# Chunk 1's inputs by sequence among the weights, block 0's state products together, and one output tile for each sequence at the end

## The chip, the cores and the metric

The kernel runs on one core of one Trainium2 chip. The metric is the device time of one execution in microseconds (us). The span of a profile is about 1.7 us shorter than the time of the same run.

Engine names: PE is TensorE (matmuls; PEld its weight loads), DVE is VectorE, ACT is ScalarE, POOL is GpSimd, SPq is SyncE's queue, which issues most DMAs.

## The reference

A chunked state-space scan (batch 4, 8 heads, 768 positions, head size 32, state size 16), whose output is the input of a feed-forward layer with the activation `h * cos(h)`:

```python
for c in range(nc):
    cum = np.cumsum(la, axis=-1)
    L = np.exp(cum[:, :, :, None] - cum[:, :, None, :]) * causal
    M = np.einsum('bhin,bhjn->bhij', Cc, Bc) * L
    y[:, :, sl] = M @ xc + (Cc @ state) * exp(cum)        # shortened
    state = decay_full * state + sum_j(Bx * decay_from_j) # shortened
...
h = x @ w_in            # (3072, 256) x (256, 2048)
g = h * np.cos(h)
return g @ w_out        # (2048, 256)
```

## The kernel before

The kernel cuts the 768 positions into 6 blocks ("chunks") of 128, each with 4 sequences. After a short prologue that scans block 0 alone, 96 steps follow, 16 for each block. In step n PE computes `hp` n (a slice of h for all four sequences), then `o` n-2 (the second matmul of the step two before). ACT and DVE make `gT` out of `hp` in between: k (ACT), w (DVE), sine (ACT), gT (DVE). The scan of the next block is woven into the steps: for each sequence `turn` (two transposes on PE, their copies cT and bcT on ACT, one product on DVE), `intra` (PE's g, DVE's m) and `finish` (PE's y, the yT copy on ACT, and the state). The weights come as words of 8 bytes and are put together on the chip in 16 pieces: `grade` (ACT and POOL), `join` (DVE and POOL).

Every engine works through its own queue in order. The two PSUM pools that matter are `bank(..., "h")` with 2 buffers for `hp`, and `pair(...)` with 2 buffers of two banks each for the scan.

```python
def load(c, each=False):                       # B, C and x of one block
    ...
    for b in range(NB if each else 1):
        ...
        for dst, src in ((bc[:, 0, rs], B), (bc[:, 1, rs], C), (xr[:, rs], x)):
            nc.sync.dma_start(out=dst, in_=src[bs, :, sl, :].rearrange("b h s n -> s (b h) n"))
...
def carry(c, b):                               # the state after block c, sequence b
    if c == NC - 1:
        return
    xr, sc = raw[c][1], scaled.pop((c, b))
    s_ps = pair("s_ps")[:, 0, 0:2 * D]         # one PSUM buffer for each sequence
    for q in range(4):
        PE.matmul(s_ps[32 * q:32 * q + 32], ...)
    state[c, b] = new = states.tile(...)
    V.tensor_tensor(out=new..., in0=s_ps..., in1=own..., op=ALU.mult)
    ...
def second(n):                                 # at the very end:
    ...
    if last:                                   # o[c] is two tiles of two sequences
        for b in range(NB):
            ob = two.tile([P, DM], FP32, tag="ob1", bufs=NB, name="ob")
            (ACT.copy if b == 1 else V.tensor_copy)(out=ob, in_=o[c][b // 2][:, b % 2])
            (nc.scalar if b % 2 else nc.sync).dma_start(out=rows_[:, b, c, :], in_=ob)
        return
...
load(1)                                        # all of chunk 1 ahead of pieces 6 to 15
load_along(1)
for b in range(NB):
    load_a(1, (b,))
    for n in (6 + 2 * b, 7 + 2 * b):
        fetch(*order[n])
...
for n in range(NC * NF + LAG):
    ...
        first(n)
        if n + 3 < len(order):
            rest = grade(*order[n + 3], later=True)
        if n + 2 < len(order):
            join(*order[n + 2])
        for b in ((0,), (1, 2), (3,))[n] if n < 3 else ():
            carry(0, b)
        gate(n)
    ...
```

Of the kernel before, what the change touches and what calls it, by code (L numbers as in the profile page):

```python
# [8 lines left out]
FP32 = mybir.dt.float32  # L9
# [16 lines left out]
def kernel(  # L26
# [22 lines left out]
    nc = tc.nc  # L49
    V, ACT, G, PE = nc.vector, nc.scalar, nc.gpsimd, nc.tensor  # L50

    NB, H, S, D = x.shape
    N = B.shape[-1]
    P = 128
    NC = S // P
    DM, DF = moe_w_in.shape
    KT = DM // P
    NF = DF // P
# [8 lines left out]
    loads = ctx.enter_context(tc.tile_pool(name="loads", bufs=3))  # L67
    rows = ctx.enter_context(tc.tile_pool(name="rows", bufs=NB))
# [10 lines left out]
    def bank(shape, name, tag):  # L79
        return psum.tile(shape, FP32, tag=tag, bufs=2, name=name)  # L80

    def pair(name):

        return psum.tile([P, 2, 4 * P], FP32, tag="scan", bufs=2, name=name)
# [13 lines left out]
    a_all = dram.tile([NB, H, S], FP32, name="a_all")  # L98
    a_cut = dram.tile([NB, H, S], FP32, name="a_cut")

    def load(c, each=False):

        if c >= NC:
            return
        sl = slice(c * P, (c + 1) * P)
        bc = loads.tile([P, 2, NB * H, N], FP32, tag="bc", name="bc")
        xr = loads.tile([P, NB * H, D], FP32, tag="xr", name="xr")
        for b in range(NB if each else 1):
            bs = slice(b, b + 1) if each else slice(0, NB)
            rs = slice(bs.start * H, bs.stop * H)  # L110
            for dst, src in ((bc[:, 0, rs], B), (bc[:, 1, rs], C), (xr[:, rs], x)):
                nc.sync.dma_start(out=dst, in_=src[bs, :, sl, :].rearrange("b h s n -> s (b h) n"))  # L112
        raw[c] = (bc, xr.rearrange("p (b h) d -> p b h d", b=NB))

    def load_a(c, seqs=range(NB)):
        if c >= NC:
            return
        for b in seqs:
            arow[c, b] = t = rows.tile([P, H, P], FP32, tag="arow", name="arow")
            nc.sync.dma_start(  # L120
                out=t, in_=a_cut[b, :, c * P:(c + 1) * P].unsqueeze(0).to_broadcast([P, H, P]))

    def load_along(c):

        if c >= NC:
            return
        along[c] = t = rows.tile([P, NB, P], FP32, tag="along", bufs=2, name="along")
        for b in range(NB):
            nc.sync.dma_start(  # L129
                out=t[:, b], in_=a_all[b, :, c * P:(c + 1) * P].unsqueeze(1)  # L130
                .to_broadcast([H, N, P]))


# [65 lines left out]
                        in1=last.rearrange("p (k f) -> p k f", k=k), op=ALU.add)  # L199

    order = [(w, i) for i in range(NPC) for w in ("in", "out")]
    load(0, each=True)
    for n in (0, 2, 1, 3, 4, 5):
        fetch(*order[n])

# [110 lines left out]
    def finish(c, b, tag=None, fills=0):  # L316
        (bcT, m), xr = part.pop((c, b)), raw[c][1]
        y = (pair("y")[:, 0] if tag is None else bank([P, 4 * P], "y", tag)
             ).rearrange("p (k i) -> p k i", k=4)
        fill(y[:, 2:4], fills)  # L320
        y = y[:, 0:2]
        if c > 0:
            s = state[c - 1, b].rearrange("p h d -> p (h d)")
            for t in range(2):
                PE.matmul(y[:, t], lhsT=s[:, t * P:(t + 1) * P], rhs=bcT[:, 1],  # L325
                          start=(t == 0), stop=False, skip_group_check=True)
        for h in range(H):
            q, t = h % 4, h // 4
            PE.matmul(y[32 * q:32 * q + 32, t], lhsT=xr[:, b, h], rhs=m[:, h],  # L329
                      start=(c == 0 and t == 0), stop=True, tile_position=(0, 32 * q),  # L330
                      skip_group_check=True)
        if b == 0:
            yT[c] = two.tile([P, 2, TB], FP32, tag="yT", name="yT")
        ACT.copy(out=yT[c][:, :, b * P:(b + 1) * P], in_=y)  # L334
        if c > 0:
            carry(c, b)

    def carry(c, b):

        if c == NC - 1:  # L340
            return
        xr, sc = raw[c][1], scaled.pop((c, b))
        s_ps = pair("s_ps")[:, 0, 0:2 * D]
        for q in range(4):
            two_ = slice(2 * q, 2 * q + 2)
            PE.matmul(s_ps[32 * q:32 * q + 32], lhsT=sc[:, two_].rearrange("p h n -> p (h n)"),  # L346
                      rhs=xr[:, b, two_].rearrange("p h d -> p (h d)"), start=True, stop=True,
                      tile_position=(0, 32 * q), skip_group_check=True)
        state[c, b] = new = states.tile([P, H, D], FP32, tag="state", name="state")
        by_two = "p (k t) d -> p k (t d)"  # L350
        V.tensor_tensor(out=new.rearrange(by_two, k=HP),
                        in0=s_ps.unsqueeze(1).to_broadcast([P, HP, 2 * D]),
                        in1=own.rearrange(by_two, k=HP), op=ALU.mult)
        if c > 0:
            V.scalar_tensor_tensor(out=new, in0=state.pop((c - 1, b)),
                                   scalar=reach[c, b][:, P - 1:P], in1=new,
                                   op0=ALU.mult, op1=ALU.add)


    hp, turns, gT, o = {}, {}, {}, {}  # L360

    def first(n):
        c, f = divmod(n, NF)
        hp[n] = bank([P, TB], "hp", "h")
        for k in range(KT):
            PE.matmul(hp[n], lhsT=w_in[:, k, f * P:(f + 1) * P], rhs=yT[c][:, k],  # L366
                      start=(k == 0), stop=(k == KT - 1))

        k = ffn.tile([P, TB], I32, tag="k", name="k")
        ACT.activation(k, hp[n], AF.Copy, bias=0.25, scale=INV_2PI)  # L370
        turns[n] = w = ffn.tile([P, TB], FP32, tag="w", name="w")
        V.scalar_tensor_tensor(out=w, in0=hp[n], scalar=INV_2PI, in1=k,  # L372
                               op0=ALU.mult, op1=ALU.subtract)
# [7 lines left out]
    def second(n):  # L381
        c, f = divmod(n, NF)
        last = c == NC - 1
        if f == 0:

            o[c] = [pair("o")[:, :, 0:DM] if last else bank([P, 2, DM], "o", "o")
                    for _ in range(2)]
        g = gT.pop(n)
        for b in range(NB):
            PE.matmul(o[c][b // 2][:, b % 2], lhsT=g[:, b * P:(b + 1) * P],  # L390
                      rhs=w_out[:, f], start=(f == 0 and (last or b % 2 == 0)),
                      stop=(f == NF - 1), skip_group_check=True)
        if f < NF - 1:
            return
        rows_ = out.rearrange("(b c p) m -> p b c m", b=NB, p=P)
        if last:
            for b in range(NB):
                ob = two.tile([P, DM], FP32, tag="ob1", bufs=NB, name="ob")
                (ACT.copy if b == 1 else V.tensor_copy)(out=ob, in_=o[c][b // 2][:, b % 2])
                (nc.scalar if b % 2 else nc.sync).dma_start(out=rows_[:, b, c, :], in_=ob)  # L400
            return
        for i in range(2):
            ob = two.tile([P, 2, DM], FP32, tag="ob", name="ob")
            (ACT.copy if i else V.tensor_copy)(out=ob, in_=o[c][i])
            nc.sync.dma_start(out=rows_[:, 2 * i:2 * i + 2, c, :], in_=ob)


# [29 lines left out]
    fill(pair("warm")[:, 0, 0:2 * P].rearrange("p (k i) -> p k i", k=2), 1)  # L437
    join(*order[2])
    join(*order[1])
    load(1)  # L440
    load_along(1)
    for b in range(NB):
        load_a(1, (b,))
        for n in (6 + 2 * b, 7 + 2 * b):
            fetch(*order[n])
# [4 lines left out]
    for n in range(NC * NF + LAG):  # L450
        c, f = divmod(n, NF)
        rest = None
        if n < NC * NF:
            if f == 0 and c > 0:
                load(c + 2)
            first(n)
            if n + 3 < len(order):
                rest = grade(*order[n + 3], later=True)
            if n + 2 < len(order):
                join(*order[n + 2])  # L460
            for b in ((0,), (1, 2), (3,))[n] if n < 3 else ():
                carry(0, b)
            gate(n)
            if rest:
                rest()
        if n >= LAG:
            second(n - LAG)
        if c + 1 < NC:
            b, j = divmod(f - 3, 3)
            if 0 <= b < NB:  # L470
                (turn, intra, finish)[j](c + 1, b)
                if j == 0:
                    decays(c + 1, b, 1)
            b, j = divmod(f - 2, 3)
            if 0 <= b < NB and j == 0:
                reaches(c + 1, b)
                decays(c + 1, b, 0)
            if f == NF - 1:
                raw.pop(c + 1)
                load_a(c + 2)  # L480
                load_along(c + 2)
# [30 lines left out]
```

## Time and profile before

| | before |
|---|---|
| time, median of 6 runs | 410.89 us (410.28 to 411.93) |
| span of the profile | 408.7 us |
| PE busy | 400.2 us, 98% |
| all waits of PE | 4.4 us, none after 41 us |
| from PE's end to the end of the span (the tail) | 4.1 us |

A row of a timeline is: start, duration, engine, line, operation, output and inputs, number of instructions, and in brackets the idle time just before and what ended it. `x4` for one `hp` are its passes. The lines that carry the argument stand in the prediction below.

To compare traces I use times from the start of `hp` 0 on, the first matmul of the 96 steps: what comes before is the same in both kernels but, as the runs show, not equally long in each execution.

### The profile page before, as it was taken

What the parts mean: (1) busy time and instruction counts of PE and PEld (TensorE: products, weight loads), DVE (VectorE), ACT (ScalarE), POOL (GpSimd) and SP (SyncE); (2) the same over time, 40 slices, a digit from 0 to 9 for tenths busy, and PEclk for the clock granted to TensorE, in tenths of its full rate; (3) what the DMA queues carried; (4) which work ended last, traced back from release to release, by engine and by line L of the source; (5) the groups of instructions that cost most, each with busy time, mean ns of one, the idle gap of its engine ahead of it and who ended that gap; (6) DMA issues with size and microseconds to landing.
All of it is one profiled execution on the core that took longest, in us unless ns stands there. A gap on an engine that the chain in (4) does not pass through costs nothing.

```text
span 408.7 us, 5526 instructions
## 1 busy us (share of the span) xinstructions
PE 400.2 (98%) x2086; PEld 262.1 (64%) x2086; DVE 267.1 (65%) x413; ACT 173.3 (42%) x328; POOL 42.7 (10%) x62
## 2 busy tenths in 40 slices
PE   8989999999999999999999999999999999999995
PEld 5636666666666766666666666666666566666664
DVE  6997999955767754777763777674576764443332
ACT  2575566534343434343344433433434343433331
POOL 2263555400000000000000000000000000000000
PEclk9999999999999999999999999999999999999999
DMA  7999994191111093110155111120100000100001
GB/s 113 303 160 298 390 180 131 47 135 54 51 52 53 0 148 84 55 36 15 54 107 75 58 47 51 51 73 6 54 0 2 0 0 2 51 0 2 0 1 52
DMA packets 106507, 30.54 MB, mean 75 GB/s; under 512 B 75184, under 2 KB 102384, under 8 KB 106480
## 3 DMA queue, kind: packets, MB, share of 16 engines
q1 hardware_dynamic: 105664, 29.66, 30.8%
q10 hardware_dynamic: 816, 0.52, 0.4%
q8 instruction: 16, 0.26, 0.3%
q14 instruction: 11, 0.09, 0.1%
HBM read 26.84 MB, written 3.34 MB: 74 GB/s over the span
## 4 chain that ended last, share of the span: by engine, by line
PE 92%; SPq 4%; DMA 1%; ACT 1%; DVE 0%; issue 0%; DVEq 0%; ACTq 0%
PE hp L366 40%; PE o L390 39%; PE g L307 4%; PE y L329 3%; SPq L112 2%; PE y L325 2%; PE a_ps L256 2%; DMA words<-in_moe_w_in_dram 1%; SPq L129 1%; PE warm L94 1%; PE tp L289 1%; PE tp L288 1%; ACT cT L293 0%; PE s_ps L346 0%; DVE lam L272 0%
## 5 line engine op out<-in xcount | busy, mean ns | idle before, releaser
L366 PE MATMUL hp<-yT,w_in 128*128 128x512 f32 x384 | 184.9, 604 | 0.5 <-DVE gT L379 0.5
L390 PEld LDWEIGHTS o<-w_out,gT 128*128 128x128 f32 x768 | 145.8, 190 | 59.6 <-issue 43.5
L390 PE MATMUL o<-w_out,gT 128*128 128x256 f32 x768 | 181.2, 379 | 0.0
L370 ACT ACTIVATE k<-hp 128x512 int32<-128x512 f32 x96 | 57.4, 597 | 126.6 <-PE hp L366 126.5
L379 DVE TENSOR_TENSOR gT<-hp,w 128x512 f32<-128x512 f32 x96 | 66.3, 690 | 66.1 <-ACT w L377 66.1
L372 DVE SCALAR_TENSOR_TENSOR w<-hp,k 128x512 f32<-128x512 f32 x96 | 66.0, 687 | 62.5 <-ACT k L370 61.2
L366 PEld LDWEIGHTS hp<-yT,w_in 128*128 128x128 f32 x384 | 67.8, 190 | 57.5 <-issue 53.7
L377 ACT ACTIVATE w<-w,quarter 128x512 f32<-128x512 f32 x96 | 69.3, 722 | 75.9 <-DVE w L372 75.9
L272 DVE TENSOR_TENSOR_SCAN lam<-arow,unit 128x512 f32<-128x512 f32 x40 | 48.4, 1211 | 0.8 <-DMA arow<-a_cut 0.8
L311 DVE TENSOR_TENSOR m<-g,lam 128x512 f32<-128x512 f32 x48 | 30.7, 681 | 0.8 <-PE g L307 0.6
L281 POOL TENSOR_TENSOR sc<-bc,lam 128x128 f32<-128x128 f32 x20 | 8.2, 412 | 200.4 <-DVE lam L272 196.4
L307 PE MATMUL g<-cT,bcT 32*128 32x256 f32 x192 | 17.4, 426 | 1.9 <-ACT bcT L295 1.9
L293 ACT ACTIVATE cT<-tp,slot 128x128 f32<-128x128 f32 x48 | 14.6, 356 | 9.3 <-PE tp L289 9.3
L329 PE MATMUL y<-m,xr 128*32 128x128 f32 x384 | 15.8, 279 | 0.2 <-DVE m L311 0.2
L307 PEld LDWEIGHTS g<-cT,bcT 32*128 32x128 f32 x192 | 7.8, 182 | 9.5 <-issue 6.2
L194 DVE SCALAR_TENSOR_TENSOR mag<-words,mag 128x512 uint32<-128x512 uint32 x16 | 13.5, 842 | 0.6
L334 ACT COPY yT<-y 128x256 f32<-128x256 f32 x24 | 8.9, 371 | 11.1 <-PE y L329 11.1
L174 POOL TENSOR_SCALAR mag<-mag 128x512 f32<-128x512 f32 x16 | 12.1, 755 | 12.8 <-ACT mag L173 12.7
L173 ACT ACTIVATE mag<-words 128x512 f32<-128x512 f32 x16 | 11.0, 685 | 4.4 <-DMA words<-in_moe_w_in_dram 4.4
L325 PEld LDWEIGHTS y<-bcT,state 128*128 128x128 f32 x80 | 12.0, 191 | 1.3 <-DVE m L311 0.3
L325 PE MATMUL y<-bcT,state 128*128 128x128 f32 x80 | 12.3, 276 | 0.0
L329 PEld LDWEIGHTS y<-m,xr 128*32 128x32 f32 x384 | 8.9, 109 | 4.3 <-DVE m L311 1.4
(48 smaller groups left out, 153.2 us busy)
## 6 DMA issues: line engine op xcount, KB each, us to landing
arow<-a_cut SPq DMA_DIRECT2D x20, 512.0 KB
words<-in_moe_w_in_dram SPq DMA_DIRECT2D x8, 512.0 KB
words<-in_moe_w_out_dram SPq DMA_DIRECT2D x8, 512.0 KB
xr<-in_x_dram SPq DMA_DIRECT2D x5, 512.0 KB
out_dram<-ob SPq DMA_DIRECT2D x10, 256.0 KB
bc<-in_B_dram SPq DMA_DIRECT2D x5, 256.0 KB
bc<-in_C_dram SPq DMA_DIRECT2D x5, 256.0 KB
along<-a_all SPq DMA_DIRECT2D x20, 64.0 KB
```

What stands on the lines that cost most here:

```text
L272: V.tensor_tensor_scan(out=lam[c, b][:, hs].rearrange("p h i -> p (h i)"), data0=rows_.rearrange("p h i -> p (h i)"), data1=unit.rearrange ...
L293: ACT.activation(cT[:, t], tp[:, 1], AF.Copy, scale=slot[:, t:t + 1])
L307: PE.matmul(g[u // 2][:, u % 2, 0:2 * P], lhsT=bcT[r, 0], rhs=cT[r].rearrange("p t i -> p (t i)"), start=True, stop=True)
L311: V.tensor_tensor(out=m[:, hs].rearrange("p (k t) i -> p k (t i)", k=2), in0=g[u][:, :, 0:2 * P], in1=l[:, hs].rearrange("p (k t) i -> p k ...
L325: PE.matmul(y[:, t], lhsT=s[:, t * P:(t + 1) * P], rhs=bcT[:, 1], start=(t == 0), stop=False, skip_group_check=True)
L329: PE.matmul(y[32 * q:32 * q + 32, t], lhsT=xr[:, b, h], rhs=m[:, h], start=(c == 0 and t == 0), stop=True, tile_position=(0, 32 * q), skip ...
L366: PE.matmul(hp[n], lhsT=w_in[:, k, f * P:(f + 1) * P], rhs=yT[c][:, k], start=(k == 0), stop=(k == KT - 1))
L370: ACT.activation(k, hp[n], AF.Copy, bias=0.25, scale=INV_2PI)
L372: V.scalar_tensor_tensor(out=w, in0=hp[n], scalar=INV_2PI, in1=k, op0=ALU.mult, op1=ALU.subtract)
L377: ACT.activation(cos, cos, AF.Sin, bias=quarter, scale=TWO_PI)
L379: V.tensor_tensor(out=gT[n], in0=hp.pop(n), in1=cos, op=ALU.mult)
L390: PE.matmul(o[c][b // 2][:, b % 2], lhsT=g[:, b * P:(b + 1) * P], rhs=w_out[:, f], start=(f == 0 and (last or b % 2 == 0)), stop=(f == NF ...
```

## The change

The intent: take away two of the waits that PE still had near the start, and shorten the tail. In three parts, cut to the core:

```diff
 # part 1: state products of block 0 together, two sequences in each PSUM buffer
+    def sum_up(c, b, s_ps):                   # the matmuls that carry() held
+        ...
+        sums[c, b] = s_ps
     def carry(c, b):
-        s_ps = pair("s_ps")[:, 0, 0:2 * D]
-        for q in range(4): ...
+        s_ps = sums.pop((c, b))
 ...
             first(n)
+            if n == 1:
+                for b in range(0, NB, 2):
+                    s_ps = pair("s_ps")
+                    for t in range(2):
+                        sum_up(0, b + t, s_ps[:, t, 0:2 * D])
 ...
-            for b in ((0,), (1, 2), (3,))[n] if n < 3 else ():
+            for b in ((0, 1), (2, 3))[n - 1] if 0 < n < 3 else ():
                 carry(0, b)

 # part 2: chunk 1 by sequence among the weights
-    load(1)
-    load_along(1)
     for b in range(NB):
+        load(1, (b, b + 1))
+        load_along(1, (b,))
         load_a(1, (b,))
         for n in (6 + 2 * b, 7 + 2 * b):
             fetch(*order[n])

 # part 3: the last block's output, one PSUM tile for each sequence,
 # copied right after that sequence's matmuls, all issued from SyncE
+            if last:
+                o[c] = [pair("o")[:, 0, 0:DM] for _ in range(2)]
+            o_ = o_full[c] = [bank([P, 2, DM], "o", "o") for _ in range(2)]
+            o[c] = (o[c] + [t[:, 0] for t in o_] if last else ...)
 ...
         for b in range(NB):
             PE.matmul(o[c][b], ...)
+            if last and f == NF - 1:
                 ob = two.tile([P, DM], FP32, tag="ob1", bufs=NB, name="ob")
-                (ACT.copy if b == 1 else V.tensor_copy)(out=ob, in_=o[c][b // 2][:, b % 2])
-                (nc.scalar if b % 2 else nc.sync).dma_start(out=rows_[:, b, c, :], in_=ob)
+                (ACT.copy if b % 2 else V.tensor_copy)(out=ob, in_=o[c][b])
+                nc.sync.dma_start(out=rows_[:, b, c, :], in_=ob)
```

More of the change, by code (lines that the diff above doesn't have):

```diff
@@ L99, with load @@
     a_cut = dram.tile([NB, H, S], FP32, name="a_cut")
-    def load(c, each=False):
+    def load(c, seqs=(0, NB)):
         if c >= NC:
             return
-        sl = slice(c * P, (c + 1) * P)
-        bc = loads.tile([P, 2, NB * H, N], FP32, tag="bc", name="bc")
-        xr = loads.tile([P, NB * H, D], FP32, tag="xr", name="xr")
-        for b in range(NB if each else 1):
-            bs = slice(b, b + 1) if each else slice(0, NB)
-            rs = slice(bs.start * H, bs.stop * H)
-            for dst, src in ((bc[:, 0, rs], B), (bc[:, 1, rs], C), (xr[:, rs], x)):
-                nc.sync.dma_start(out=dst, in_=src[bs, :, sl, :].rearrange("b h s n -> s (b h) n"))
-        raw[c] = (bc, xr.rearrange("p (b h) d -> p b h d", b=NB))
+        if c not in raw:
+            raw[c] = (loads.tile([P, 2, NB * H, N], FP32, tag="bc", name="bc"),
+                      loads.tile([P, NB, H, D], FP32, tag="xr", name="xr"))
+        bc, xr = raw[c]
+        xr = xr.rearrange("p b h d -> p (b h) d")
+        rs = slice(seqs[0] * H, seqs[1] * H)
+        for dst, src in ((bc[:, 0, rs], B), (bc[:, 1, rs], C), (xr[:, rs], x)):
+            nc.sync.dma_start(out=dst, in_=src[seqs[0]:seqs[1], :, c * P:(c + 1) * P, :]
+                              .rearrange("b h s n -> s (b h) n"))
     def load_a(c, seqs=range(NB)):
@@ L121, in load_a, with load_along @@
                 out=t, in_=a_cut[b, :, c * P:(c + 1) * P].unsqueeze(0).to_broadcast([P, H, P]))
-    def load_along(c):
+    def load_along(c, seqs=range(NB)):
         if c >= NC:
             return
-        along[c] = t = rows.tile([P, NB, P], FP32, tag="along", bufs=2, name="along")
-        for b in range(NB):
+        if c not in along:
+            along[c] = rows.tile([P, NB, P], FP32, tag="along", bufs=2, name="along")
+        for b in seqs:
             nc.sync.dma_start(
-                out=t[:, b], in_=a_all[b, :, c * P:(c + 1) * P].unsqueeze(1)
+                out=along[c][:, b], in_=a_all[b, :, c * P:(c + 1) * P].unsqueeze(1)
                 .to_broadcast([H, N, P]))
@@ L201 @@
     order = [(w, i) for i in range(NPC) for w in ("in", "out")]
-    load(0, each=True)
+    for b in range(NB):
+        load(0, (b, b + 1))
     for n in (0, 2, 1, 3, 4, 5):
@@ L334, in finish @@
         ACT.copy(out=yT[c][:, :, b * P:(b + 1) * P], in_=y)
-        if c > 0:
+        if 0 < c < NC - 1:
+            sum_up(c, b, pair("s_ps")[:, 0, 0:2 * D])
             carry(c, b)
-    def carry(c, b):
-        if c == NC - 1:
-            return
+    sums = {}
+    def sum_up(c, b, s_ps):
         xr, sc = raw[c][1], scaled.pop((c, b))
-        s_ps = pair("s_ps")[:, 0, 0:2 * D]
         for q in range(4):
@@ L348, in carry @@
                       tile_position=(0, 32 * q), skip_group_check=True)
+        sums[c, b] = s_ps
+    def carry(c, b):
+        s_ps = sums.pop((c, b))
         state[c, b] = new = states.tile([P, H, D], FP32, tag="state", name="state")
@@ L357, in carry @@
                                    op0=ALU.mult, op1=ALU.add)
-    hp, turns, gT, o = {}, {}, {}, {}
+    hp, turns, gT, o, o_full = {}, {}, {}, {}, {}
     def first(n):
@@ L384, in second @@
         if f == 0:
-            o[c] = [pair("o")[:, :, 0:DM] if last else bank([P, 2, DM], "o", "o")
-                    for _ in range(2)]
+            if last:
+                o[c] = [pair("o")[:, 0, 0:DM] for _ in range(2)]
+            o_ = o_full[c] = [bank([P, 2, DM], "o", "o") for _ in range(2)]
+            o[c] = (o[c] + [t[:, 0] for t in o_] if last else
+                    [t[:, i] for t in o_ for i in range(2)])
         g = gT.pop(n)
+        rows_ = out.rearrange("(b c p) m -> p b c m", b=NB, p=P)
         for b in range(NB):
-            PE.matmul(o[c][b // 2][:, b % 2], lhsT=g[:, b * P:(b + 1) * P],
+            PE.matmul(o[c][b], lhsT=g[:, b * P:(b + 1) * P],
                       rhs=w_out[:, f], start=(f == 0 and (last or b % 2 == 0)),
                       stop=(f == NF - 1), skip_group_check=True)
-        if f < NF - 1:
-            return
-        rows_ = out.rearrange("(b c p) m -> p b c m", b=NB, p=P)
-        if last:
-            for b in range(NB):
+            if last and f == NF - 1:
                 ob = two.tile([P, DM], FP32, tag="ob1", bufs=NB, name="ob")
-                (ACT.copy if b == 1 else V.tensor_copy)(out=ob, in_=o[c][b // 2][:, b % 2])
-                (nc.scalar if b % 2 else nc.sync).dma_start(out=rows_[:, b, c, :], in_=ob)
+                (ACT.copy if b % 2 else V.tensor_copy)(out=ob, in_=o[c][b])
+                nc.sync.dma_start(out=rows_[:, b, c, :], in_=ob)
+        if last or f < NF - 1:
             return
@@ L403, in second @@
             ob = two.tile([P, 2, DM], FP32, tag="ob", name="ob")
-            (ACT.copy if i else V.tensor_copy)(out=ob, in_=o[c][i])
+            (ACT.copy if i else V.tensor_copy)(out=ob, in_=o_full[c][i])
             nc.sync.dma_start(out=rows_[:, 2 * i:2 * i + 2, c, :], in_=ob)
```

## The prediction

> **What bounds the kernel now.** I read the page's busy table first: TensorE (PE) is the engine to look at.
>
> ```profile
> PE 400.2 (98%) x2086; PEld 262.1 (64%) x2086; DVE 267.1 (65%) x413; ACT 173.3 (42%) x328; POOL 42.7 (10%) x62
> ```
>
> The waits of PE come next. They are all it ever waited for in 408.7 us; the windows say that none lies after 41 us (PE is busy 309.00 of the 309.00 us from 90 to 399), so that the middle of the kernel can't be shortened by moving instructions.
>
> ```profile
> PE g L307 <- ACT bcT L295: 1.9, 3, 0.9
> PE warm L94 <- DVE quarter L210: 1.1, 1, 1.1
> PE s_ps L346 <- DVE state L351: 0.7, 1, 0.7
> PE hp L366 <- DVE gT L379: 0.5, 1, 0.5
> PE y L329 <- DVE m L311: 0.2, 1, 0.2
> ```
>
> Together 4.4 us, and 4.1 us of tail after PE's end at 404.6. Then PE's timeline in the stretch that the change touches; the columns are start, duration, what, and the idle time just before.
>
> ```profile
> 22.41 1.95 PE L366 MATMUL hp<-yT,w_in 128*128 128x512 f32 x4
> 24.30 0.32 PE L346 MATMUL s_ps<-xr,sc 128*32 128x64 f32 x8
> 24.55 1.98 PE L366 MATMUL hp<-yT,w_in 128*128 128x512 f32 x4
> 26.46 0.43 PE L346 MATMUL s_ps<-xr,sc 128*32 128x64 f32 x16
> 27.36 1.95 PE L366 MATMUL hp<-yT,w_in 128*128 128x512 f32 x4 [0.46 <-DVE gT L379]
> 30.01 0.32 PE L346 MATMUL s_ps<-xr,sc 128*32 128x64 f32 x8 [0.70 <-DVE state L351]
> 30.26 1.99 PE L390 MATMUL o<-w_out,gT 128*128 128x256 f32 x8
> 32.09 1.88 PE L366 MATMUL hp<-yT,w_in 128*128 128x512 f32 x4
> ...
> 37.47 1.89 PE L390 MATMUL o<-w_out,gT 128*128 128x256 f32 x8
> 40.10 1.03 PE L307 MATMUL g<-cT,bcT 32*128 32x256 f32 x8 [0.74 <-ACT bcT L295]
> ```
>
> The reader is to see two holes: the fourth sequence's state product (30.01) has no free PSUM buffer until VectorE (DVE) has read the earlier ones, and the first `o` stands behind it; and the first g of chunk 1 (40.10) waits for ScalarE (ACT). ACT's timeline says why ACT is late:
>
> ```profile
> 37.51 0.69 ACT L173 ACTIVATE mag<-words 128x512 f32<-128x512 f32 x1 [2.85 <-DMA words<-in_moe_w_in_dram]
> ```
>
> and the SyncE queue why those words are late: their issue stands behind the whole of chunk 1.
>
> ```profile
> 17.25 7.01 SPq L112 DMA_DIRECT2D bc<-in_C_dram  x1
> 24.31 2.39 SPq L112 DMA_DIRECT2D xr<-in_x_dram  x1
> 26.80 4.29 SPq L129 DMA_DIRECT2D along<-a_all  x4
> 31.13 0.46 SPq L120 DMA_DIRECT2D arow<-a_cut  x1
> 31.64 1.13 SPq L159 DMA_DIRECT2D words<-in_moe_w_in_dram  x1
> ```
>
> Last, the tail:
>
> ```profile
> 403.77 0.42 DVE L399 COPY ob<-o 128x256 f32<-128x256 f32 x1 [1.46 <-PE o L390]
> 404.23 0.37 ACT L399 COPY ob<-o 128x256 f32<-128x256 f32 x1 [2.64 <-DVE ob L399]
> 404.63 0.76 DVE L399 COPY ob<-o 128x256 f32<-128x256 f32 x2 [0.44 <-PE o L390]
> ```
>
> **What the Trainium skill says.** "Perfetto Trace Analysis", section "Identifying the Most-Contended Engine", warns that matmul busy time is no measure of the distance to the roofline, since matmuls are pipelined. Agreed, so I work with start-to-start times: in the plain stretch near the end one step (`hp` 387.20, `o` 388.92, next `hp` 390.65) takes 3.45 us, 1.72 for each half. "DMA: Bandwidth & Descriptors", section "Why small descriptors are slow (HBM only)", has a fixed cost for each packet. The trace agrees: over 22 to 27 us, while B and C in 64-byte rows move, the finely sliced DMA row shows 24 to 197 GB/s, against 309 to 395 when weights move. The same page, section "Two DMAs through the same engine are not ordered", says that a DMA which reads what another wrote has to wait for that one's semaphore before it is issued; the built order shows just that wait on the first `along`, which reads a_all. "PSUM — Partial Sum Buffer", section "PSUM bank collisions raise a hardware error", says that ACT and DVE must not read one bank at a time. In the tail ACT's copy started at 404.23, right after DVE's ended (403.77 + 0.42 = 404.19), though the two halves of that tile lie in different banks: the wait guards the tile, not the bank.
>
> **Part 1: all state products of block 0 together.** Nothing is added or removed: 32 passes of s_ps and four state updates on DVE. They now stand between the second and third `hp`, two sequences in each PSUM tile, so two tiles suffice and no product waits for DVE. Walk it from `hp` 0 at 22.41, whose start does not change. `hp` 1 follows at once, 22.41 + 1.72 = 24.13 instead of 24.55. The 32 passes (0.43 us for 16) then take about 0.9, to some 26.8. `hp` 2 needs the PSUM bank that gT 0 releases, and gT 0 hangs on `hp` 0 by k, w, sine and gT (24.41, 25.04, 25.76, 26.52 in the trace), none of which the change touches. So `hp` 2 stays at 27.36: moving work ahead of it gains nothing. After it, though, `o` 0 can start at 27.36 + 1.72 = 29.08 instead of 30.26, and ends at 30.80. `hp` 3 waits for gT 1, which DVE computes at 30.21 to 30.89; DVE's work before it since 27.58 is the same (w, two steps of the weight join, two updates, gT). With 0.15 from gT to matmul, as at 27.21 and 27.36, `hp` 3 starts at 31.05 instead of 32.09: **1.05 us gained**. Of the 1.18 that `o` 0 gains, 0.13 is lost again to gT 1.
>
> **Part 2: chunk 1's inputs by sequence.** The bytes are the same; 3 loads become 12, each a quarter, and `along` goes one by one. Before the seventh piece of weights now stand 1024 rows each of B, C and x instead of 4096, one `along` instead of four. The DMA backlog of the first weights ends near 21.5. A quarter of the 7.5 us that B, C and x took is 1.9; then one `along` (about 0.5) after a_all has landed, one `arow` (512 KB, 1.6) and the piece (1.5): an estimate from these rates is 28 to 30, instead of 37.43, against a need at about 33.6. So the 2.85 us wait of ACT goes, and with it the 0.76 us that DVE's first decay scan waited for its `arow` at 34.97. What is left is DVE's own queue. It has one more update now (0.37) before gT 2, so: gT 2 to 33.9, reach to 34.4, scan (1.15 net) to 35.6, w 3 to 36.2, join to 37.0, gT 3 to 37.7. ACT: sine 3 to 37.0, the second half of the weight step to 37.6, cT to 38.1, bcT to 38.25. PE: `hp` 3 31.05, `o` 1 32.77, two transposes 34.49, `hp` 4 34.71, `o` 2 36.43, ends 38.15, so g starts at 38.2 to 38.5 instead of 40.10. **1.6 to 1.9 us in all at this point, of which part 1 gave 1.05**: so part 2 adds 0.55 to 0.85.
>
> From 41 to 82 DVE is nearly full (43.48 of 48.94 us for 41 to 90, and its only repeated waits are 0.36 each 12.5 us), so a gain that PE has must be matched by DVE: its next scan moves from 40.29 to about 38.6, 1.7. I take 1.65 for the front.
>
> **Part 3: the last outputs.** One tile for each sequence; copies alternate DVE, ACT, DVE, ACT, right after each sequence's four matmuls, which end 0.43 apart (403.32, 403.75, 404.18, 404.61). The copies no longer queue: before, the last ran 405.01 to 405.39 on DVE behind the third. Now it runs 404.63 to 405.00 on ACT. The issues, all on SyncE, take 0.35 each in the trace and are 0.43 apart, so they fit. The last leaves 0.38 earlier: **0.36 us**. All transfers after it stay as they are.
>
> Sum: 1.65 + 0.36 = 2.0 of the 410.9 us measured: **408.9 us**.
>
> **Rivals.**
> - *DVE takes the place of the removed waits.* For it: DVE is busy 9.5 of each 10 us between 40 and 80, and it gets 0.37 more before gT 2; joins sometimes take 0.98 or 1.64 instead of 0.69. If the scans of chunk 1 then hold up m and y, half of the front's gain is lost: about 409.8. Against it: DVE idles 2.3 us of 30 to 40 in waits that go.
> - *The loads are hidden or get worse.* The first `along` blocks the whole SyncE queue until a_all has landed. If that is as late as the old issue at 26.80, the weights come at 31 to 32, still in time. If small loads pay more each (0.6 us of issue, twelve times) later pieces come late, and PE waits once more near 50: about 410.5. Against: issue time is 7.8 us in place of the 10.2 that the three loads took.
> - *The gain is absorbed later.* PE shows no wait after 41 us that an earlier start could fill; so what is gained at 41 should stay. If gains do vanish, only the tail is left: 410.5.
> - *More than that:* if the scan and the first g move up by all of their waits, 2.3 in front and 0.4 behind give 408.2.
>
> **Range and chances.** The first and last rival bound the likely cases, 408.2 to 409.8; runs of the same kernel spread 0.5 us, so I take 408.1 to 410.2. 2% is 8.2 us, twice all PE waits: faster 0.01, same 0.98, slower 0.01.
>
> **What would show it.** Right: s_ps in one row of 32 before `hp` 2, `hp` 2 still waiting for gT until about 27.36, `o` 0 near 29.1, `hp` 3 near 31.05, ACT's wait for words gone, first g near 38.3, four tail copies in turn between 403.3 and 405.0 on a clock shifted by the front's gain. Wrong: `hp` 2 moved, a new PE wait for m or gT between 40 and 80, ACT or DVE still waiting for DMA at 33 to 36, or SyncE's last issue as long after PE's end as before.

## The result, and the profile after

The changed kernel took 408.22 us (median of 6 runs, 407.81 to 408.68) against 410.89. The ratio is 0.9935, with a 95% interval of 0.992 to 0.9949. A ratio here is the mean time of one kernel's fast runs over that of the other's of the same rounds, so not quite the ratio of the medians. Executions over 1.5% slower than the fastest of the same kernel are left out of the means. It is the same within 2%, as predicted, and lies near the lower end of the predicted range: 2.7 us were gained where 2.0 were forecast.

PE's busy time hardly moved; what changed is when it could start.

```profile
PE 400.0 (98%) x2086; PEld 262.5 (65%) x2086; DVE 266.3 (65%) x412; ACT 173.5 (43%) x329; POOL 43.6 (11%) x62
```

PE's waits in the changed kernel (us in total, times, longest):

```profile
PE g L309 <- ACT bcT L297: 1.2, 2, 0.9
PE warm L94 <- DVE quarter L212: 1.1, 1, 1.1
PE hp L373 <- DVE gT L386: 0.7, 1, 0.7
PE y L331 <- DVE m L313: 0.2, 1, 0.2
```

The wait of s_ps for DVE is gone, and of the three waits of g for bcT the one in chunk 1 (0.74) is gone; the two left lie in the prologue. The wait of `hp` for gT grew from 0.5 to 0.7. PE's timeline from `hp` 0 on:

```profile
23.14 3.67 PE L373 MATMUL hp<-yT,w_in 128*128 128x512 f32 x8
26.74 0.65 PE L348 MATMUL s_ps<-xr,sc 128*32 128x64 f32 x32
28.08 1.96 PE L373 MATMUL hp<-yT,w_in 128*128 128x512 f32 x4 [0.69 <-DVE gT L386]
29.87 1.89 PE L401 MATMUL o<-w_out,gT 128*128 128x256 f32 x8
31.65 1.98 PE L373 MATMUL hp<-yT,w_in 128*128 128x512 f32 x4
...
38.96 0.73 PE L309 MATMUL g<-cT,bcT 32*128 32x256 f32 x8
39.62 1.98 PE L373 MATMUL hp<-yT,w_in 128*128 128x512 f32 x4
```

| us after the start of `hp` 0 | before | after | gained |
|---|---|---|---|
| `hp` 2 | 4.95 | 4.94 | 0.01 |
| `o` 0 | 7.85 | 6.73 | 1.12 |
| `hp` 3 | 9.68 | 8.51 | 1.17 |
| first g of chunk 1 | 17.69 | 15.82 | 1.87 |
| `hp` 5 | 18.65 | 16.48 | 2.17 |
| PE's end | 382.18 | 380.06 | 2.12 |
| and the tail after it | 4.11 | 3.50 | 0.61 |

So 2.12 + 0.61 = 2.73 us from `hp` 0 on, which agrees with the 2.67 between the medians. (A profile prints its span to 0.1 us, so every tail given here is good to 0.05; by the unrounded times of the traces these two are 4.12 and 3.54, a gain of 0.58.) The two spans differ by 2.0 only (408.7 and 406.7), because `hp` 0 started at 23.14 in this profile and at 22.41 in the other; the experiments show what that is.

On ACT the seventh piece of weights is no longer waited for; the row has no bracket:

```profile
34.23 0.67 ACT L174 ACTIVATE mag<-words 128x512 f32<-128x512 f32 x1
```

On SyncE's queue that piece is issued at 24.54, where it was 31.64:

```profile
16.92 3.40 SPq L112 DMA_DIRECT2D bc<-in_C_dram  x1
20.37 2.69 SPq L112 DMA_DIRECT2D xr<-in_x_dram  x1
23.27 0.73 SPq L130 DMA_DIRECT2D along<-a_all  x1
24.11 0.37 SPq L120 DMA_DIRECT2D arow<-a_cut  x1
24.54 0.57 SPq L160 DMA_DIRECT2D words<-in_moe_w_in_dram  x1
```

And in the tail the copies alternate, each right after its own matmuls, none behind another engine's:

```profile
402.38 0.37 ACT L406 COPY ob<-o 128x256 f32<-128x256 f32 x1 [2.18 <-PE o L401]
402.40 1.83 SPq L407 DMA_DIRECT2D out_dram<-ob  x4
402.81 0.42 DVE L406 COPY ob<-o 128x256 f32<-128x256 f32 x1 [0.44 <-PE o L401]
403.24 0.37 ACT L406 COPY ob<-o 128x256 f32<-128x256 f32 x1 [0.49 <-PE o L401]
```

### The profile page after: what moved, and what is told of

Its sections match the earlier page's. It is cut to its first block, busy times and chain, and to the rows that moved or that the text cites. A ratio compares the mean times of both kernels' runs of the same rounds, so it can differ in the third digit from the quotient of the medians.

```text
span 406.7 us, 5538 instructions
## 1 busy us (share of the span) xinstructions
PE 400.0 (98%) x2086; PEld 262.5 (65%) x2086; DVE 266.3 (65%) x412; ACT 173.5 (43%) x329; POOL 43.6 (11%) x62
## 4 chain that ended last, share of the span: by engine, by line
PE 94%; SPq 2%; DMA 1%; ACT 1%; DVE 1%; issue 0%; DVEq 0%
PE hp L373 42%; PE o L401 41%; PE g L309 4%; PE y L331 3%; PE y L327 2%; SPq L112 2%; DMA words<-in_moe_w_in_dram 1%; PE tp L290 1%; PE tp L291 1%; PE s_ps L348 0%; PE y L94 0%; ACT w L384 0%; DVE m L313 0%; DVE w L379 0%; DVE gT L386 0%
## 5 line engine op out<-in xcount | busy, mean ns | idle before, releaser
L295 ACT ACTIVATE cT<-tp,slot 128x128 f32<-128x128 f32 x48 | 14.6, 354 | 10.0 <-PE tp L291 10.0
L331 PE MATMUL y<-m,xr 128*32 128x128 f32 x384 | 15.8, 279 | 0.2 <-DVE m L313 0.2
```

What stands on the lines that cost most here:

```text
L295: ACT.activation(cT[:, t], tp[:, 1], AF.Copy, scale=slot[:, t:t + 1])
L331: PE.matmul(y[32 * q:32 * q + 32, t], lhsT=xr[:, b, h], rhs=m[:, h], start=(c == 0 and t == 0), stop=True, tile_position=(0, 32 * q), skip ...
```

## The experiments

The question after the result is not whether, but how: do the parts' gains simply add, as the prediction's sum has it, or do they need each other? And what made the tail worth 0.61 instead of 0.36? Twelve kernels ran (one of them the changed kernel again), in three groups; the columns are the times with their ratio to the kernel before of the same rounds, and the trace of one run each, from `hp` 0 on.

| kernel | median, us | ratio (95%) | `hp` 0 at | `hp` 3 | `hp` 5 | PE's end | tail |
|---|---|---|---|---|---|---|---|
| before | | | 22.41 | 9.68 | 18.65 | 382.18 | 4.11 |
| part 1 alone | 411.27 | 0.9994 (0.9964 to 1.0023) | 24.39 | 8.51 | 17.61 | 381.53 | 4.18 |
| part 2 alone | 409.83 | 0.9961 (0.9939 to 0.9983) | 23.20 | 9.69 | 17.53 | 380.88 | 4.02 |
| part 3 alone | 410.39 | 0.9981 (0.9954 to 1.0007) | 22.81 | 9.68 | 18.08 | 381.62 | 3.57 |
| parts 1 and 2 | 408.73 | 0.9932 (0.9914 to 0.9950) | 23.38 | 8.50 | 16.47 | 380.07 | 4.25 |
| words first | 412.65 | 1.0052 (0.9997 to 1.0106) | 23.76 | 9.69 | 18.75 | 382.33 | 4.11 |
| first sequence only | 408.84 | 0.9932 (0.9899 to 0.9964) | 23.32 | 8.52 | 16.49 | 382.05 | 3.43 |
| changed, tail on two queues | 408.59 | 0.9933 (0.9905 to 0.9961) | 23.58 | 8.51 | 16.50 | 380.07 | 3.85 |
| before, tail on SyncE | 410.79 | 0.9988 (0.9962 to 1.0014) | 22.70 | 9.69 | 19.13 | 383.06 | 3.84 |
| changed, again | 407.93 | 0.9929 (0.9916 to 0.9941) | 22.43 | 8.51 | 16.50 | 380.10 | 3.57 |
| first words early | 408.12 | 0.9928 (0.9914 to 0.9943) | 22.70 | 8.52 | 16.50 | 380.08 | 3.52 |
| third bank | 408.72 | 0.9951 (0.9933 to 0.9969) | 23.01 | 7.73 | 16.86 | 380.45 | 3.54 |
| both | 407.91 | 0.9929 (0.9916 to 0.9941) | 22.13 | 7.73 | 16.86 | 380.44 | 3.53 |

All outputs were correct. The longest runs had the lowest clocks: those of 412.5 us and more, of all kernels here, show 0.991 to 0.996.

### One part at a time

The theory of the prediction is that the steps add: part 1 gives 1.05 us, part 2 the rest. Its rival: the first g of chunk 1 is a gate that opens when the DMA has brought its data, whatever PE does before, and then part 1 alone can't gain.

The edits are the parts of the diff above, each put into the kernel before by itself.

> The kernel before with part 1 alone (state products of block 0 together). Measure: from the start of hp 0 to the start of hp 5, 18.65 us before and 16.48 after. Theory 'steps add' (as in the prediction: part 1 gives 1.05 us by itself): hp 3 at 8.5 us after hp 0, hp 5 at about 17.5, time about 409.8. Theory 'gate': the seventh piece of weights still lands at 37 us, and ACT, which waits for it in order, still releases the first g at 40; hp 3 moves to 8.5 after hp 0 as well, but PE then waits longer before g, hp 5 stays within 0.2 us of 18.65, and the time stays at 410.7 to 411.0.

> The kernel before with part 2 alone (chunk 1 by sequence among the weights). Steps add: part 2 gives 0.55 to 0.85 us, time about 410.1, hp 5 at about 17.9 after hp 0. Gate: hp 3 stays at 9.7 after hp 0, PE then runs without a gap through o 2 and g, hp 5 at about 17.4 (1.2 us gained), time about 409.7; ACT's wait for words and DVE's wait for arow gone.

> The kernel before with part 3 alone (one output tile for each sequence, all issues on SyncE). From PE's end to the end of the span 4.11 us before, 3.50 after. Prediction: 0.36 us gained (3.75 left), time 410.5. If the whole 0.6 us of the changed kernel is the tail's own: 3.5 us left, time 410.3. Front as before, 18.65.

> Parts 1 and 2 without the tail. Both theories: front as in the changed kernel, hp 5 at 16.5 after hp 0, tail 4.1 us; time 408.7 to 408.9 if the tail is worth 0.6, 408.6 if 0.36. Steps add: the gain over before is the sum of the two parts' own gains; gate: it is clearly more than the sum (about 2.1 against 0 + 1.2).

Part 1 alone moved `hp` 3 just as in the changed kernel (8.51), and the time by 0.06%, with an interval that spans zero. The 1.05 us of the prediction, 0.26%, lie inside that interval too, so the times decide nothing. In its trace these are ACT's two waits for weights:

```profile
16.92 0.66 ACT L173 ACTIVATE mag<-words 128x512 f32<-128x512 f32 x1 [4.61 <-DMA words<-in_moe_w_in_dram]
38.47 0.68 ACT L173 ACTIVATE mag<-words 128x512 f32<-128x512 f32 x1 [2.89 <-DMA words<-in_moe_w_in_dram]
```

and this is PE's wait at the first g:

```profile
41.04 1.03 PE L307 MATMUL g<-cT,bcT 32*128 32x256 f32 x8 [0.77 <-ACT bcT L295]
```

From the start of ACT's `mag` to g it is 41.04 - 38.47 = 2.57 us. In the three other traces with chunk 1 in bulk ahead of those words it is 40.10 - 37.51 = 2.59 (before), 39.94 - 37.36 = 2.58 (part 3 alone) and 40.87 - 38.30 = 2.57 (before with the tail on SyncE). That is the gate: g follows the landing of the seventh piece at a fixed distance, which ACT fills without a gap (`mag`, sine, `last`, cT, bcT), and what PE has saved before it is waited away. The trace of part 1 alone still shows 1.04 us less from `hp` 0 to `hp` 5 than before, but only because `hp` 0 was late in it (24.39); in absolute time its g came later (41.04 after 40.10). My expectation of 18.65 after `hp` 0 missed that: the gate is fixed to the DMA, not to `hp` 0. By the yardstick set before the run, the 17.61 speaks for the steps that add (17.5); the reading as a gate came after it, from the rows above.

Part 2 alone left `hp` 3 where it was (9.69) and moved `hp` 5 by 1.12 and PE's end by 382.18 - 380.88 = 1.30; the expectation of the gate was 1.2. With it in place, part 1 adds 380.88 - 380.07 = 0.81. By the times alone the two don't clearly exceed their sum (0.06% and 0.39% against 0.68%, with intervals of some 0.2 to 0.3% each); what settles it is the gate in the traces. Part 3 alone shortened the tail to 3.57; its time, 0.19% with an interval that includes 0, is too small to be resolved by itself. With part 3 left out the tail was 4.25 and the rest as in the changed kernel, near what both theories said.

### Does it take the words, the scan's rows, or both?

The kernel before, with the words ahead of chunk 1 and nothing split:

```diff
+    for n in (6, 7):
+        fetch(*order[n])
     load(1)
     load_along(1)
     for b in range(NB):
         load_a(1, (b,))
-        for n in (6 + 2 * b, 7 + 2 * b):
+        for n in (6 + 2 * b, 7 + 2 * b) if b else ():
             fetch(*order[n])
```

> The kernel before, only the seventh and eighth piece of weights issued ahead of chunk 1's loads; nothing split. If ACT's wait for words alone held the first g (rival), that wait goes, hp 5 comes about 1 us earlier (17.7 after hp 0), time about 409.9. If it takes words and arow together, since DVE too works in order: arow lands some 3 us later than at 34.97, DVE's first scan waits about 3 to 4 us for it instead of 0.76, the first g comes 1 to 2 us later than before, hp 5 at 19.7 to 20.7 after hp 0, time about 412 to 413.

ACT's wait is gone from its trace, and DVE waits for its rows instead:

```profile
37.70 1.22 DVE L272 TENSOR_TENSOR_SCAN lam<-arow,unit 128x512 f32<-128x512 f32 x1 [2.14 <-DMA arow<-a_cut]
```

That wait was 0.76 before. `hp` 5 came 18.75 after `hp` 0, no better than before (18.65), where 17.7 would have shown that the words alone were in the way. That yardstick is coarse (with the same front it was 18.08 and 19.13 in two other traces), but PE itself still waited 0.84 for bcT at g, against 0.74 before. So the rival falls: one late transfer had hidden another. The size was off: I had expected a wait of 3 to 4 us and `hp` 5 a full 1 to 2 us later. The time, 412.65 with a ratio of 1.0052, is at the edge of its interval, and one of the four runs took 416.51 at a clock of 0.991, so I read no more from it than that nothing was gained.

Then the changed kernel with only the first sequence by itself:

```diff
-        load(1, (b, b + 1))
-        load_along(1, (b,))
+        if b < 2:
+            load(1, ((0, 1), (1, NB))[b])
+            load_along(1, ((0,), range(1, NB))[b])
```

> The changed kernel, but only chunk 1's first sequence is loaded by itself; the other three come in one load each of B, C and x behind the eighth piece of weights. If what counts is that the first sequence's inputs and the seventh piece come before the bulk: hp 5 at 16.5 after hp 0 as changed. The bulk of 9216 rows then holds up the ninth piece, by about 5 us to some 41 to 43; ACT needs it near 42: so the gain may be kept, or up to 1 us of it lost to a wait for words one or two steps later. If the even split of all four is needed, PE shows a wait after hp 5 and the time is 0.5 to 2 us above the changed kernel's 408.2.

Up to `hp` 5 it ran as the changed kernel (16.49). After that ACT waited for the ninth piece:

```profile
46.58 0.67 ACT L174 ACTIVATE mag<-words 128x512 f32<-128x512 f32 x1 [3.88 <-DMA words<-in_moe_w_in_dram]
```

and PE waited 0.22 at the next transposes and 0.91 at the next g; by PE's end the front's whole gain was lost (382.05 after `hp` 0). So in this trace the even split of all four sequences matters as well. But this profile fell on the slowest of the four runs (410.49; the others took 407.65 to 409.25), and their median, 408.84, doesn't differ clearly from the changed kernel. Whether each run loses that much stays open.

### What made the tail shorter

Part 3 does two things: it frees the copies from each other, and it issues all of the last outputs from SyncE. Each can be done without the other, in one line.

```diff
 # the changed kernel, tail on two queues
-                nc.sync.dma_start(out=rows_[:, b, c, :], in_=ob)
+                (nc.scalar if b % 2 else nc.sync).dma_start(out=rows_[:, b, c, :], in_=ob)
 # the kernel before, tail on SyncE
-                (nc.scalar if b % 2 else nc.sync).dma_start(out=rows_[:, b, c, :], in_=ob)
+                nc.sync.dma_start(out=rows_[:, b, c, :], in_=ob)
```

> The changed kernel, odd sequences' outputs issued from ScalarE's queue as before. From PE's end to the end 3.50 us in the changed kernel, 4.11 before. If the earlier copy is all that counts, 3.5 to 3.6 remains (or a bit less, as the issues overlap). If the queue counts too (the last transfer of before ran from ScalarE's queue, and its data ended later after its issue), about 3.75 to 3.9.

> The kernel before, all last outputs issued from SyncE. If the queue counts: 3.8 to 3.9 us from PE's end to the end, instead of 4.11. If only the copies count: 4.1. Front 18.65 as before; time 410.6 to 410.9.

| tail, us | two queues | SyncE alone |
|---|---|---|
| copies as before | 4.11 | 3.84 |
| one tile for each sequence | 3.85 | 3.50 |

Each half is worth some 0.3 us (0.27 to 0.31 by the unrounded times), and they about add up. The split shows why: from PE's end to the end of the last issue, then from there to the end of the span.

| | last issue ends | then to the end |
|---|---|---|
| before | 1.17 | 2.94 |
| before, tail on SyncE | 1.45 | 2.39 |
| changed, tail on two queues | 0.78 | 3.07 |
| changed | 1.03 | 2.47 |

All on one queue, the last issue ends 0.25 to 0.28 later (fourth of four in line, not second of two), but the wait after it is some 0.55 shorter. Over all traces it is 2.4 to 2.6 where SyncE issued last (8 traces) and 2.8 to 3.1 where ScalarE's queue did (6 traces). What lengthens it shows in the DMA queues of the tail. The columns are packets, MB, and share of 16 engines' time; q1 is SyncE's queue and q10 ScalarE's. First the kernel before, from 404 us on,

```profile
q1 hardware_dynamic: 288, 0.26, 16.0%
q10 hardware_dynamic: 288, 0.26, 16.0%
q14 instruction: 1, 0.01, 0.8%
```

then the changed kernel, from 402 us on:

```profile
q1 hardware_dynamic: 576, 0.52, 31.9%
```

One packet on q14, 8192 bytes of instructions, fell into the first tail and not into the second. The packet times in the traces show what it did. In all six traces with ScalarE's queue it ended 1.73 to 2.12 us after PE's end, and nine of the last 144 packets of each queue, a sixteenth, began only then, the first within 0.02 us of its end. The other 135 of ScalarE's last issue were done 1.03 to 1.05 us after that issue's end, those nine 1.56 to 1.72 after it. In the eight traces with SyncE alone the instruction packet came 3.8 us or more after PE's end, behind everything; there the first 135 were done 0.95 after the last issue, and all 144 1.01 to 1.02. So the queue itself accounts for 0.1 us at most. The rest is one sixteenth of the packets, by its size the share of one of the 16 DMA engines, held up behind a fetch of instructions. Why the fetch falls there when ScalarE issues, and whose instructions it brings, no run here shows. The times of these two kernels (0.9933 and 0.9988) don't resolve 0.3 us; the verdict rests on the traces.

### Can more be had?

The changed kernel still waits 0.69 us before `hp` 2 for gT 0, and ACT still waits in the prologue for the first piece of weights. Two edits aim at these, a third does both, and the changed kernel ran beside them.

```diff
 # first words early
     for b in range(NB):
         load(0, (b, b + 1))
-    for n in (0, 2, 1, 3, 4, 5):
+        if b == 1:
+            fetch(*order[0])
+    for n in (2, 1, 3, 4, 5):
         fetch(*order[n])
 # third bank: hp 2 in a scan buffer, all four state products in the other
-        hp[n] = bank([P, TB], "hp", "h")
+        hp[n] = pair("hp")[:, 0] if n == 2 else bank([P, TB], "hp", "h")
 ...
-                for b in range(0, NB, 2):
-                    s_ps = pair("s_ps")
-                    for t in range(2):
-                        sum_up(0, b + t, s_ps[:, t, 0:2 * D])
+                s_ps = pair("s_ps")
+                for b in range(NB):
+                    sum_up(0, b, s_ps[:, b // 2, b % 2 * 2 * D:(b % 2 + 1) * 2 * D])
```

> The changed kernel once more, as the yardstick for the three beside it. hp 0 anywhere from 22.4 to 24.4 us, as the first piece of weights lands; from hp 0 to PE's end 380.06 us and 3.50 us of tail, as in its first trace, since neither depends on that landing; time 407.9 to 408.7, ratio to before 0.993.

> The changed kernel with the first piece of weights issued after the second sequence of chunk 0 instead of after the fourth: the same idea as part 2, in block 0. In ten traces so far ACT waited 0.8 to 4.6 us for that piece, PE up to 2.8 us behind it, and hp 0 started anywhere from 22.4 to 24.4. If that wait sets the start of hp 0: ACT's wait for the first words gone, hp 0 at 22.0 to 22.5 each time, time 0.5 to 1 us below the changed kernel beside it, and a narrower spread. Rival: sequence 2 and 3 now land later, and PE waits for their transposes: hp 0 not earlier, time equal or up to 1 us worse.

> The changed kernel with all four state products in one PSUM tile, and the third hp in the tile thus freed, so that it needs no bank that gT 0 releases. hp 2 starts at about 4.3 after hp 0 instead of 4.94, hp 3 at 7.8 instead of 8.51. If PE's bank wait is what counts there, hp 5 comes 0.7 us earlier (15.8 after hp 0). If DVE's in-order queue, full from w 1 to the bcT of chunk 1, is the bound by now, g comes at about 15.5 instead of 15.82 behind a new wait of 0.5 us for bcT, and 0.3 us or less is gained.

> Both of the two above. Their gains lie in different stretches and should add: 0.8 to 1.3 us below the changed kernel beside it, 407.0 to 407.5, if both hold.

The changed kernel repeated itself: 380.10 from `hp` 0 to PE's end, 3.57 of tail, 0.9929.

The third bank did what was asked on PE: `hp` 2 at 4.18 with no wait, `hp` 3 at 7.73, 0.78 earlier than in the changed kernel. By the first g all of it was gone:

```profile
38.92 1.03 PE L309 MATMUL g<-cT,bcT 32*128 32x256 f32 x8 [0.62 <-ACT bcT L297]
```

g came 15.91 after `hp` 0, against 15.82, and as it then took 1.03 instead of 0.73, `hp` 5 came 0.36 later than in the changed kernel. bcT is a copy on ACT behind the sine of step 3, which waits for w 3 from DVE, and DVE's queue was full from w 1 (28.17) to gT 3 (38.54): it had no gap longer than 0.05 us, and no earlier matmul can empty it. So from here on DVE is what sets g, as the first rival of the prediction had it, though only one step beyond this change. I had expected g at 15.5 even so. The rest was lost in one instruction: DVE's first scan (`lam`) started 11.73 after `hp` 0, as in the changed kernel (11.70), but took 1.56 instead of 1.19. POOL's `mag` had begun 0.19 before it; in the changed kernel it began 0.14 after the scan, and there POOL's took 1.46 instead of 0.67. The second trace of each (both; changed, again) shows the same, but no run was made to show that the overlap is the cause. The time was no better (0.9951 beside 0.9929, with intervals that overlap).

The early first words took ACT's wait away, and won nothing: 0.9928. The 14 traces show what sets the start of `hp` 0. In nine of the twelve where ACT waited for the first words, `hp` 0 came 7.47 to 7.54 us after ACT's `mag` on those words (for part 1 alone 24.39 - 16.92). In the other five it came 14.44 or 14.45 after the first transpose: in three whose wait for the words was the shortest of the twelve, 0.82 to 1.59 (the kernel before, the one with its tail on SyncE, the third bank), and in the two with the words early. So the later of two chains starts the steps: the one from the first weights, or PE's own prologue. The first transpose waits for no load in these traces. It follows 24 passes of a_ps without a gap, and these start 0.21 us apart until a moment that differs, and 0.11 apart from then on: in part 1 alone from the first pass, in the changed kernel after some 7.1 us. So the transpose started anywhere from 7.04 to 8.56, and the `mag`, where it waited, from 14.34 to 16.92. Moving the words forward removes one wait and leaves the other chain: its `hp` 0 at 22.70 is 8.26 + 14.44. No version clearly beat the changed kernel; doing both gave 407.91 beside 407.93.

## Why the prediction was right

Range and class held. By its own steps:

- **`hp` 2 does not move.** Right: 4.95 and 4.94 after `hp` 0. PE had more of its work done before it and waited 0.69 instead of 0.46.
- **`o` 0 and `hp` 3.** Right: predicted gain at `hp` 3 1.05, measured 1.17. `hp` 3 started 0.06 after gT 1's end (30.92 + 0.67 = 31.59, then 31.65), not the 0.15 after it that I had copied from another place; it also stood 1.78 behind `o` 0, where a plain half step is 1.72, so at most 0.06 of the predicted 0.13 was lost to gT 1.
- **The words arrive in time.** Right: no wait of ACT or DVE for a DMA between 20 and 60 us in the changed kernel. Whether they landed at 28 to 30, as estimated, the views do not show.
- **The first g.** Right: predicted 15.8 to 16.1 after `hp` 0, measured 15.82.
- **The front as a whole, 1.65.** Too small; it was 2.12. Two terms were off. I took the low part of my own 1.6 to 1.9, out of care for DVE, and DVE kept up: its bcT product moved from 40.08 to 38.64. And I stopped the count at the start of g. The g of before was itself slow, 0.96 from its start to `hp` 5 against 0.66 after. Its second half waits for DVE's product out of the same PSUM buffer, which before began at 40.08 and lasted 0.29, while g had begun at 40.10; afterwards the product began at 38.64 and was over before g at 38.96:

  ```profile
  40.08 0.29 DVE L297 TENSOR_TENSOR bcT<-tp,reach 128x128 f32<-128x128 f32 x1 [0.54 <-ACT bcT L295]
  38.64 0.29 DVE L299 TENSOR_TENSOR bcT<-tp,reach 128x128 f32<-128x128 f32 x1 [0.37 <-ACT bcT L297]
  ```

  That is 0.3 that no line of the waits shows as idle, because the matmul row simply gets longer (1.03 against 0.73).
- **"Part 1 gave 1.05, so part 2 adds 0.55 to 0.85."** The sum at g was right, the sharing out was not. Part 1 alone gained nothing that the times resolve (0.06%), part 2 alone 1.30 in the trace, and part 1 is worth 0.81 on top of it. A gain before a gate counts only once the gate has been moved.
- **The tail, 0.36.** Too small; it was 0.61. The copy was sized right (its end 0.80 after PE's end before, 0.41 after). But the last issue left only 0.14 earlier, not 0.38: SyncE had to take all four. That "all transfers after it stay as they are" was wrong: what follows the last issue became 0.47 shorter (2.94 to 2.47), since the instruction fetch that held up one DMA engine no longer fell into it.
- **Sum.** 2.0 predicted; 2.12 + 0.61 = 2.73 in the traces, 2.67 between medians. Some of this is luck: both terms were too small, and 408.22 lies only 0.12 inside the range. That the class would be "same" was nearly certain, as all waits together were half of 2%.
- **The rivals.** DVE did not take the waits' place in this change, but did in the next one (third bank). The small loads brought no new wait, but not for the reason given: their twelve issues held SyncE for 24.1 us in sum, not the 7.8 predicted (0.6 each). "More than that", 408.2, came nearest. Nothing was absorbed later: 2.17 at `hp` 5, 2.12 at PE's end.

## What to carry to other kernels

When PE waits twice in a row, ask of the second wait whether it hangs on PE's own progress or on an arrival in absolute time: if it is an arrival, removing the first wait alone gains nothing, and the two changes have to be judged together. Interleave loads in the order of need when one late transfer holds an in-order engine, and check what else that engine's neighbours wait for, or the next late transfer takes its place. Compare traces from a common event inside the kernel, not from the span's start, when the changes are smaller than the variation of the start. When one queue seems slower than another, look for a packet of a third queue among its own before calling it slow.

## What the Trainium skill lacked or had wrong

- "DMA: Bandwidth & Descriptors", section "Issuing engines are not separate DMA queues", says that issuing from several engines only saves sequencer time. The packets here nearly agree: the 135 of 144 that nothing held up were done 1.03 to 1.05 us after the last issue from ScalarE and 0.95 from SyncE. What no page gives is how long an instruction fetch can hold up other transfers on its DMA engine: here an 8192-byte packet on q14 moved the end of the last output by 0.5 to 0.7 us.
- "Perfetto Trace Analysis", section "DMA Instruction — HWDGE (DVE, Sync)", says that a DMA engine may begin before all descriptors are made if they do not fit in the buffer, but gives no size of it. Here an issue of 4096 rows behind another such one held SyncE for 7.01 us in the kernel before, an issue of 1024 rows in the changed kernel for 3.40 or less (C) and up to 3.92 (x); a page that gave the number of rows would let such stalls be worked out.
- No page says how far the arrival of the first transfers varies from run to run. Here ACT's first work on weights, where it waited for them, started between 14.34 and 16.92 us over twelve traces of kernels with the same first issues, and `hp` 0 between 22.41 and 24.39.
